# Raw first weights of the later pairs of feature tiles loaded behind the third chunk's attention output

## The chip, the cores and the metric

The kernel runs on one core of one Trainium2 chip. The metric is the device time of one execution in microseconds (us), and the median of several executions is compared. Five engines work side by side, each on its own list of instructions in a fixed order: PE (TensorE: matrix products, with PEld for its weight loads), DVE (VectorE), ACT (ScalarE), POOL (GpSimd) and SP (SyncE). POOL and SP mainly issue transfers (DMA) here, each on a queue of its own.

## What is computed

Two identical layers, one after the other, on a sequence of 2048 positions of width 576. Each layer is sliding dilated attention (32 heads of 18, 8 keys at distance 2) and a feed-forward part with SiLU over 4608 hidden features, each with a layer norm ahead and a residual around it. Both layers use the same weights.

```python
qkv = (x @ wqkv)                                   # 576 -> 3*576, 32 heads of 18
idx = pos[:, None] - arange(8)[None, :] * 2        # 8 keys, every second position back
logits = einsum("bhsd,bhswd->bhsw", q, k[idx]) * 18**-0.5   # masked where idx < 0
o = einsum("bhsw,bhswd->bhsd", softmax(logits), v[idx])
A(x) = o @ wo
B(x) = silu(x @ w1) @ w2                           # 576 -> 4608 -> 576
x = x + A(layernorm(x));  x = x + B(layernorm(x))  # layer 1
x = x + A(layernorm(x));  x = x + B(layernorm(x))  # layer 2
```

## The kernel before

**Chunks and stages.** The positions are cut into four chunks of 512, so that two layers make eight steps, `s` = 0 to 7 (`s` = 2 is the third chunk of the first layer). A step has an attention (four units of 8 heads, mostly DVE work: products L837 and L870, sums L841 and L877/L878, softmax L850 to L857), a projection with `wo`, and a feed-forward part.

**The projection** (`project`) takes the attention output `o` in four tiles of 128 positions. DVE writes each as two fp16 parts (L898 the high one, L492 the low one) into a buffer `yh`, of which there are two. From step 2 on SP then turns the tile with a transposing transfer (L509) into `oT`, shown as `yo`, of which there are two as well. The list `flipped` collects these turns. PE multiplies each turned tile with `wo` in two halves (L925), each into one of three PSUM banks (`z0`, `z1`, `misc0`), and DVE adds a half to the residual (L927), which frees the bank.

**The feed-forward part** of the first two chunks works on 36 single feature tiles: a product per tile (L1385, 14 matmuls into one of the same three banks), SiLU and split on ACT and DVE (L1387, L1389, L1392), and a second product per two tiles (L1345, four blocks of 12 weight steps). From the third chunk on the tiles are taken in 18 pairs with a fast form of the first product (`ffn_pairs`, L1232): seven products a pair instead of eight. For it the input is first made into seven forms (`forms`, L1179 to L1203), and the first weights of each pair into seven sums and differences in two fp16 parts.

**Making these weights** is `prepare(q)`, once for each of 18 pairs. POOL loads the raw weights of the pair with eight transfers (L1072, L1076; 768 KB) into one of two buffers `wr` (shown as `wq`). DVE forms four sums (L1083), ACT writes the high parts (L1091), DVE the low parts (L1098), and POOL stores both blocks of the pair into `wfs` in device memory (L1103). SP later reads `wfs` back, seven transfers per pair and chunk (L1108).

**What sets the order.** The program is first collected as operations, each with an engine, an estimated duration, what it reads and writes, a priority (lower goes first) and possibly operations that it must come after (`after=`). `Plan.order()` then plays this through with estimated durations and buffers and writes down one fixed order, which all engines follow. Priorities are mostly the step number: feed-forward work on DVE has `s - 0.5`, the attention `s - 1.0`, and `prepare` has `PREP = 0.9`, that is behind the second chunk's feed-forward work (0.5) and ahead of the third chunk's attention (1.0). Within the loop over steps, `front(s + 1)` records the attention, the projection and the forms of the next step.

Of the kernel before, what the change touches and what calls it, by code (L numbers as in the profile page):

```python
# [17 lines left out]
P = 128  # L18
# [23 lines left out]
NP = NFT // 2  # L42
# [4 lines left out]
W2N = 11  # L47
FAR = 6
PREP = 0.9
PS = 0.45  # L50
S2 = 2
TWICE = {6: 0, 7: 0}
# [22 lines left out]
class Plan:  # L75
# [18 lines left out]
    def op(self, eng, dur, fn, reads=(), writes=(), prio=0.0, nbytes=0, table=None, after=(), lanes=1, lag=0.0):  # L94
        o = Op()
        o.lag = lag
        o.eng, o.dur, o.fn, o.prio, o.seq, o.nbytes, o.table = eng, dur, fn, prio, len(self.ops), nbytes, table
        o.outs, o.end, o.lanes = [], None, lanes
        deps = set(after)
        for k in reads:  # L100
            if k in self.writer:
                deps.add(self.writer[k])
        for k in writes:
            if k in self.writer:
                deps.add(self.writer[k])
            deps.update(self.readers.get(k, ()))
        for k in reads:
            self.readers.setdefault(k, []).append(o)
        for k in writes:
            self.writer[k] = o  # L110
            self.readers[k] = []
        deps.discard(o)
        o.deps = deps
        o.n = len(deps)
        for d in deps:
            d.outs.append(o)
        o.bufs = []
        for k in (*reads, *writes):
            b = k[0] if isinstance(k, tuple) else k
            if isinstance(b, Buf) and b not in o.bufs:  # L120
                o.bufs.append(b)
                b.left += 1
                if b.turn is None:
                    b.turn = self.named[b.tag]
                    self.named[b.tag] += 1
        self.ops.append(o)
        return o
# [152 lines left out]
def sliding_attention_silu_ffn(ctx: ExitStack, tc: tile.TileContext, x, wqkv, wo, w1, w2, out):  # L280
# [6 lines left out]
    op = S.op  # L287

    def fl(t):
        return t.rearrange("p a b -> p (a b)")  # L290
# [8 lines left out]
    def T(b):  # L299
        if isinstance(b, tuple):  # L300
            return T(b[0])[:, b[1]]
        return S.tags[b.tag][b.slot]
# [152 lines left out]
    wsc = accw[:, 0:NP, :]  # L455
# [65 lines left out]
    turned, held, flipped = [], [], []  # L521
# [539 lines left out]
            nc.vector.tensor_scalar(dz, r12.rearrange("p (q f) i -> p q f i", f=2)[:, :, 0, 0], 2.0 / LNX, None, op0=ALU.mult)  # L1061
        op("DVE", 1.0, fn, [("s12", f) for f in range(NFT)] + [("sh", 2, g) for g in range(len(G2))], ["wsc"], -0.5)

    def prepare(q, prio):

        w, v = Buf("wr"), Buf("ws")

        def load():
            t = T(w)
            for h in range(2):  # L1070
                for k in range(2):
                    nc.gpsimd.dma_start(t[:, h:4:2, k, :], w1[h * KH + k * P:h * KH + (k + 1) * P, 2 * q * P:(2 * q + 2) * P].rearrange(  # L1072
                        "p (f c) -> p f c", f=2))
                for f in range(2):
                    v = w1[h * KH + 2 * P:(h + 1) * KH, (2 * q + f) * P:(2 * q + f + 1) * P]
                    nc.gpsimd.dma_start(t[:, h + 2 * f, 2, :], bass.AP(tensor=v.tensor, offset=v.offset, ap=[[0, 4], *v.ap]))  # L1076
        op("POOL", 4.8, load, ["wsc"], [w], prio, nbytes=P * 12 * P * 4, lanes=8)

        def sums():
            t, u = T(w), T(v)  # L1080
            for o, a, b, f in ((u[:, 0], t[:, 2], t[:, 3], ALU.add), (u[:, 1], u[:, 0], t[:, 0], ALU.subtract),
                               (t[:, 2], t[:, 0], t[:, 2], ALU.subtract), (u[:, 2], t[:, 1], u[:, 1], ALU.subtract)):
                nc.vector.tensor_tensor(o, a, b, op=f)  # L1083
        op("DVE", 2.0, sums, [w], [w, v], prio)
        for x, r0, r1, g in ((w, 0, 4, Buf("wg")), (v, 4, 7, Buf("wh"))):
            n = r1 - r0

            def hi(x=x, g=g):
                d, t = T(g), T(x)
                for k0, k1, c in ((0, 2, 0), (2, 3, 1)):  # L1090
                    nc.scalar.activation(d[:, :, k0:k1, :].rearrange("p a b c -> p a (b c)"),  # L1091
                                         t[:, :, k0:k1, :].rearrange("p a b c -> p a (b c)"), AF.Copy, scale=wsc[:, q, c:c + 1])
            op("ACT", 0.4 * n, hi, [x, "wsc"], [(g, 0)], prio)

            def lo(x=x, g=g):
                d, t = T(g), T(x)
                for o, k0, k1 in ((3, 0, 2), (2, 2, 3)):
                    nc.vector.scalar_tensor_tensor(  # L1098
                        d[:, :, o:o + k1 - k0, :].rearrange("p a b c -> p a (b c)"),
                        t[:, :, k0:k1, :].rearrange("p a b c -> p a (b c)"), wsc[:, q, 0:1],  # L1100
                        d[:, :, k0:k1, :].rearrange("p a b c -> p a (b c)"), op0=ALU.mult, op1=ALU.subtract)
            op("DVE", 0.43 * n, lo, [x, (g, 0)], [(g, 0)], prio)
            op("POOL", 0.57, lambda g=g, r0=r0, r1=r1: nc.gpsimd.dma_start(  # L1103
                wfs[q][:, r0 * KB:r1 * KB], T(g).rearrange("p i a b -> p (i a b)")), [(g, 0)], [("wfs", q, r0 // 4)], prio, nbytes=P * n * KB * 2)
# [347 lines left out]
    def load_x(s, prio, ahead=None, spilt=False, into=None):  # L1452

        lay, c = divmod(s, NC)
        halves = [Buf("x") for _ in range(2)] if into is None else [Buf(into)]
        xs = [(halves[j // 2], j % 2) if into is None else (halves[0], j) for j in range(NJ)]
        for j in range(NJ):
            src = (lambda j=j: x_rows(x, c, j)) if lay == 0 else (lambda j=j: (xe if spilt else xd)[c][j])
            if ahead and lay == 0:
                op("POOL", 0.54, lambda j=j, src=src: nc.gpsimd.dma_start(T(xs[j]), src()), [], [xs[j]], prio,  # L1460
                   nbytes=P * D * 4, after=ahead)
            else:
                op("SP", 0.41, lambda j=j, src=src: nc.sync.dma_start(T(xs[j]), src()), [("xe" if spilt else "xd", c, j)] if lay else [],
                   [xs[j]], prio, nbytes=P * D * (4 if s else 5), after=ahead or ())
        return xs
# [3 lines left out]
    def front(s):  # L1469
        X[s] = load_x(s, s - 1.0 if s else -20)  # L1470
        if s == 0:
            no_keys()
            xT = layer_norm(X[0], -20, "xa", 3, PE_LN[0])
            x1 = layer_norm(load_x(1, -8.5, gate[0:1]), -8.5, "xb", False, PE_LN[1])
            x2 = layer_norm(load_x(2, -2.0, gate[3:4]), -2.0, "xb", True, PE_LN[2])

            def more(u, w):
                qkv_ahead(1, u, x1, w)
                qkv_ahead(2, u, x2, w)
                ahead.append((u, w))  # L1480
            o = attention(0, xT, raw_wq, more)
            x3 = layer_norm(load_x(3, -1.2, gate[11:12]), -1.2, "xa", 2, PE_LN[3])
            for u in (2, 0, 1, 3):
                store_wq(u, ahead[u][1], PACE_WQ[u])
            for u in (0, 1, 3, 2):
                qkv_ahead(3, u, x3, ahead[u][1] if u != 2 else load_wq(2, -0.95))
            raw_wo()
        else:
            o = attention(s, None, None)
        project(s, o, X[s])  # L1490
        XT[s] = layer_norm(X[s], s - 1.0, "xb", s == 1, s == 0) if s < S2 else forms(X[s], s - 1.0, ("ya", "yc"))
# [25 lines left out]
    def turn(s):  # L1517
        XT[s] = forms(load_x(s, s - 1.0, spilt=True), s - 1.0, into="ye")
        X[s] = load_x(s, s - 1.0, spilt=True)
# [14 lines left out]
    for s in range(NL * NC):  # L1534

        if s < S2:
            ffn(s, XT[s], X[s])
        else:
            ffn_pairs(s, XT[s], X[s], TWICE.get(s, len(G2)))
        if s == 0:  # L1540
            for q in range(NP):
                prepare(q, PREP)
        if s == 2:
            op("POOL", 0.55, lambda: nc.gpsimd.dma_start(wos, fl(T(WO))), [(WO, k) for k in range(10)], ["wos"], 2.0, nbytes=P * 20 * D, after=flipped[-1:])
        if 2 <= s < NC:
            layer_norm(X[s], AN[s + NC] + 0.0, None, False, own=True, keep=xn[s - 2])
        if s < NC - 1:
            front(s + 1)
        if s == NC - 1:
            norm(NC)  # L1550
            attend(NC)
            norm(NC + 1)
            turn(NC)
            attend(NC + 1)
            norm(NC + 2)
            attend(NC + 2)
            norm(NC + 3)
        if NC <= s < NL * NC - 1:
            turn(s + 1)
        if s == NC:  # L1560
            attend(NC + 3)
            for q in range(NP):
                prepare_second(q, NC + 1 + PS, attended[-1:])
    for o in S.order():
# [28 lines left out]
```

## Time and profile before

| what | value |
|---|---|
| median of 3 runs | 2123.3 us (2121.58 to 2124.65) |
| profiled execution, own time | 2119.38 us |
| its span in the trace | 2117.6 us |
| PE busy | 2088.3 us, 99% of the span |
| DVE busy | 1754.9 us, 83% |
| ACT busy | 1025.8 us, 48% |
| POOL busy | 388.5 us, 18% |
| transfers | 489.07 MB, 231 GB/s |

The profiled execution's own time is 1.78 us above its span, and 3.9 us below the median of the timed runs. A row of a timeline gives the start, the duration, the engine, the line, the operation, what it writes `<-` what it reads, the count, and in brackets the idle time of the engine just before it and what ended it. SPq, DVEq and the like are the queues that issue an engine's instructions.

### The profile page before, as it was taken

To read this page: it belongs to the slowest core of one execution; us is meant where nothing else is said; L and a number is where in the kernel's file an instruction comes from. 1 tells how busy PE (TensorE), PEld (TensorE's weight loads), DVE (VectorE), ACT (ScalarE), POOL (GpSimd) and SP (SyncE) were. 2 spreads that over 40 slices of the span, in tenths; PEclk is the share of its full clock that TensorE was granted. 3 is DMA by queue.
4 is the path that set the end of the run, shared out by engine and by line. 5 is a ranking of instruction groups with operands and counts; after the bars stand their busy time and mean duration, and the time that the engine had idled before them with its cause. 6 is when DMAs were issued, how large, how long until landed. Compare 5 with 4: busy or idle time off the path is not lost.

```text
span 2117.6 us, 41751 instructions
## 1 busy us (share of the span) xinstructions
PE 2088.3 (99%) x16017; PEld 1539.5 (73%) x16017; DVE 1754.9 (83%) x2861; ACT 1025.8 (48%) x1857; POOL 388.5 (18%) x628
## 2 busy tenths in 40 slices
PE   8999999999999999999999999999999999999999
PEld 4556556665566888877786777777788888888887
DVE  8899999999876998679997978986996748766665
ACT  7555787644345454434434433434444545444442
POOL 2133566343322232011111001001000000000000
PEclk9999999999999999999999999999999999999999
DMA  6477777687989889886677896786989999779772
GB/s 188 146 212 256 236 258 248 214 243 221 250 206 297 264 275 252 210 261 189 177 220 208 218 273 195 217 225 185 247 256 302 330 258 290 218 213 272 221 210 76
DMA packets 377632, 489.07 MB, mean 231 GB/s; under 512 B 150600, under 2 KB 300724, under 8 KB 373080
## 3 DMA queue, kind: packets, MB, share of 16 engines
q1 hardware_dynamic: 332456, 336.85, 56.9%
q0 software_dynamic: 42960, 148.45, 21.8%
q8 instruction: 125, 2.05, 0.4%
q10 hardware_dynamic: 2016, 1.11, 0.2%
q14 instruction: 75, 0.61, 0.1%
HBM read 350.96 MB, written 86.85 MB: 207 GB/s over the span
## 4 chain that ended last, share of the span: by engine, by line
PE 87%; DVE 6%; DMA 4%; ACT 1%; issue 1%; SPq 0%; POOL 0%; ACTq 0%; DVEq 0%
PE acc L1345 19%; PE z L1232 16%; PE misc L1232 10%; PE z L735 9%; PE acc L1322 9%; PE z L1385 7%; PE acc L1409 4%; PE misc L1345 4%; PE misc L735 3%; PE z L925 3%; PE misc L1385 2%; PE misc L925 1%; DMA kvs<-kvs 1%; DMA yo<-yh 1%; DVE prs L837 1%
## 5 line engine op out<-in xcount | busy, mean ns | idle before, releaser
L1232 PEld LDWEIGHTS <-w 128*128 128x128 f16 x5292 | 516.5, 98 | 74.5 <-issue 2.5
L1345 PE MATMUL acc<-w,h 128*128 128x320 f16 (+2 forms) x3780 | 548.2, 280 | 2.3 <-DVE x L1353 2.3
L1345 PEld LDWEIGHTS <-h 128*128 128x128 f16 x4320 | 407.6, 98 | 122.3 <-issue 3.3
L1232 PE MATMUL z<-xb,w 128*128 128x256 f16 x3213 | 405.0, 273 | 0.5 <-DVE wq L1239 0.5
L1232 PE MATMUL misc<-xb,w 128*128 128x256 f16 x2079 | 272.2, 273 | 1.1 <-DVE wq L1239 0.8
L735 PEld LDWEIGHTS <-xa 128*128 128x128 f16 x1344 | 130.8, 98 | 115.5 <-issue 6.7
L837 DVE TENSOR_TENSOR prs<-qts,kvs 128x2304 f32<-128x2304 f32 x64 | 163.4, 2554 | 18.8 <-DMA kvs<-kvs 17.0
L870 DVE TENSOR_TENSOR prs<-kvs,pe 128x1152 f32<-128x1152 f32 x128 | 170.3, 1352 | 1.0
L841 DVE TENSOR_REDUCE lg<-prs 128x128 f32<-128x2304 f32 x64 | 163.1, 2548 | 0.9
L735 PE MATMUL z<-wq,xa 128*128 128x432 f16 x840 | 160.2, 346 | 2.1 <-ACT h L748 2.1
L1345 PE MATMUL misc<-w,h 128*128 128x384 f16 x540 | 139.7, 326 | 0.0
L877 DVE TENSOR_TENSOR prs<-prs 128x1152 f32<-128x1152 f32 (+1 forms) x128 | 135.1, 1056 | 3.2
L1331 DVE SCALAR_TENSOR_TENSOR x<-acc,d2x,x 128x576 f32<-128x576 f32 (+1 forms) x85 | 68.7, 810 | 57.2 <-PE acc L1322 56.6
L1385 PEld LDWEIGHTS <-w 128*128 128x128 f16 x588 | 57.9, 99 | 74.2 <-issue 7.6
L1409 PE MATMUL acc<-w,h 128*128 128x288 f16 x864 | 108.4, 286 | 1.9 <-DVE h L1392 1.1
L1409 PEld LDWEIGHTS <-h 128*128 128x128 f16 x864 | 83.7, 98 | 25.2 <-DVE h L1392 1.4
L1385 PE MATMUL z<-xb,w 128*128 128x512 f16 x420 | 93.9, 379 | 0.7 <-DVE w L1011 0.6
L1385 PE MATMUL z<-xb,wq 128*128 128x512 f16 x420 | 92.8, 379 | 1.7 <-ACT h L1387 1.7
L1236 ACT ACTIVATE wq<-z 128x256 f32<-128x256 f32 x107 | 40.8, 382 | 103.8 <-PE z L1232 103.7
L1387 ACT ACTIVATE h<-z,d 128x512 f32<-128x512 f32 x60 | 40.9, 682 | 94.9 <-PE z L1385 86.4
L1322 PEld LDWEIGHTS <-h 128*128 128x128 f16 x756 | 74.0, 98 | 17.6
L925 PEld LDWEIGHTS <-yo 128*128 128x128 f16 x672 | 65.7, 98 | 18.6 <-issue 1.9
(322 smaller groups left out, 3369.0 us busy)
## 6 DMA issues: line engine op xcount, KB each, us to landing
w<-wfs SPq DMA_DIRECT2D x756, 160.0 KB, 3.9
w<-w2s SPq DMA_DIRECT2D x180, 288.0 KB, 4.9
wq<-wqs SPq DMA_DIRECT2D x17, 1080.0 KB, 6.6
kvs<-kd POOLq DMA_DIRECT2D x8, 1584.0 KB, 8.4
w<-w1s SPq DMA_DIRECT2D x36, 320.0 KB, 5.9
wfs<-xa POOLq DMA_DIRECT2D x18, 640.0 KB, 4.6
kvs<-wts SPq DMA_DIRECT2D x80, 144.0 KB, 3.1
w2s<-w POOLq DMA_DIRECT2D x36, 288.0 KB, 4.7
```

Of the source, the lines that this page charges most:

```text
L735: nc.tensor.matmul(T(m)[:, :3 * UC], a, b, start=n == 0, stop=n == len(pl) - 1)
L837: nc.vector.tensor_tensor(T(pr), T(qt)[:, j:j + 2, None, :].to_broadcast([P, 2, W, UC]), win(T(kv), j, 2), op=ALU.mult)
L841: nc.vector.tensor_reduce(T(lg)[:, j:j + 2].rearrange("p a w h -> p (a w h)"), T(pr).rearrange("p a w (h d) -> p (a w h) d", d=DH), axis=A ...
L870: nc.vector.tensor_tensor(T(pr)[:, a].rearrange("p w (h d) -> p w h d", d=DH), v, T(pe)[:, j + a, :, :, None].to_broadcast([P, W, UH, DH]) ...
L877: nc.vector.tensor_tensor(t[:, :, 0:h, :], t[:, :, 0:h, :], t[:, :, h:2 * h, :], op=ALU.add)
L925: nc.tensor.matmul(T(m)[:, 0:288], a, b, start=n == 0, stop=n == len(pl) - 1)
L1232: nc.tensor.matmul(t, w[:, u, :], v[:, r, :], start=first and m == 0, stop=m == 6, skip_group_check=True)
L1322: nc.tensor.matmul(T(acc)[:, j, 0:KH], T(hb[t])[:, a, row[k], j * P:(j + 1) * P], T(wb[k, t])[:, w, :], start=k in (5, 1, 2) and t == 0 an ...
L1331: nc.vector.scalar_tensor_tensor(v, T(acc)[:, a:b, 0:KH], d2x[:, g:g + 1], v, op0=ALU.mult, op1=ALU.add)
L1345: nc.tensor.matmul(T(fa[b])[:, o:o + 2 * n].rearrange("p (a b) -> p a b", a=2), h(f, a, j), w(f)[:, :, v, c:c + n], start=q == f == m == 0 ...
L1385: nc.tensor.matmul(T(z), v, u, start=m == 0, stop=m == len(pl) - 1)
L1409: nc.tensor.matmul(T(acc)[:, h, 0:288], T(hb[q])[:, a, j * P:(j + 1) * P], T(wbs[q][0])[:, h, w, :], start=q == 0 and m == 0, stop=q == n ...
```

## The change

A constant `HELD = 5` is new. `prepare` gets a parameter `after` that is handed to its loading operation. Pairs 0 to 4 are recorded where all 18 were. Pairs 5 to 17 are recorded one step later, behind the third chunk's `front(2)`, and their load on POOL must come after `flipped[-1]`, which is then the turn of the fourth tile of the third chunk's attention output. Priority and all else of `prepare` stay.

```diff
+HELD = 5
...
-    def prepare(q, prio):
+    def prepare(q, prio, after=()):
...
-        op("POOL", 4.8, load, ["wsc"], [w], prio, nbytes=P * 12 * P * 4, lanes=8)
+        op("POOL", 4.8, load, ["wsc"], [w], prio, nbytes=P * 12 * P * 4, lanes=8, after=after)
...
         if s == 0:
-            for q in range(NP):
+            for q in range(HELD):
                 prepare(q, PREP)
...
         if s < NC - 1:
             front(s + 1)
+        if s == 1:
+            for q in range(HELD, NP):
+                prepare(q, PREP, flipped[-1:])
```

Lines of the changed kernel stand one higher than before from the constant on. Since the order is planned, one new dependence moves instructions on every engine. Three places show it.

DVE, at the end of the third chunk's attention (`prs` holds the weighted values, `xa` the prepared weights, `yh` the first tile for the projection). Before:

```order
L870 TENSOR_TENSOR prs<-kvs,pe_82 128x1152 x2
L1098 SCALAR_TENSOR_TENSOR xa<-wq,accw,xa 128x4x256
L1098 SCALAR_TENSOR_TENSOR xa<-wq,accw,xa 128x4x128
L1098 SCALAR_TENSOR_TENSOR xa<-wq,accw,xa 128x3x256
L1098 SCALAR_TENSOR_TENSOR xa<-wq,accw,xa 128x3x128
L877 TENSOR_TENSOR prs<-prs 128x2x576
L877 TENSOR_TENSOR prs<-prs 128x2x288
L878 TENSOR_TENSOR o<-prs 128x2x144
L898 TENSOR_SCALAR yh<-o,so 128x576
```

Now, at the same place:

```order
L871 TENSOR_TENSOR prs<-kvs,pe_82 128x1152 x2
L878 TENSOR_TENSOR prs<-prs 128x2x576
L878 TENSOR_TENSOR prs<-prs 128x2x288
L879 TENSOR_TENSOR o<-prs 128x2x144
L899 TENSOR_SCALAR yh<-o,so 128x576
L871 TENSOR_TENSOR prs<-kvs,pe_82 128x1152 x2
L878 TENSOR_TENSOR prs<-prs 128x2x576
L878 TENSOR_TENSOR prs<-prs 128x2x288
L879 TENSOR_TENSOR o<-prs 128x2x144
L493 SCALAR_TENSOR_TENSOR yh<-o,so,yh 128x512
L493 SCALAR_TENSOR_TENSOR yh<-o,so,yh 128x64
L899 TENSOR_SCALAR yh<-o,so 128x576
```

The four low parts of pair 5 are gone from here, and so are its four sums a little earlier; both now stand behind the projection.

POOL, in the same stretch (`wfs_218` and `wfs_219` are the prepared weights of pairs 4 and 5, `kd_275` and `kd_276` the keys and values of the fourth chunk's first two units, `qd` their queries). Before, with the raw loads of pairs 4 and 5 ahead of it and those of pairs 6 and 7 behind it:

```order
L1103 DMA wfs_218<-xa 128x2560
L1103 DMA wfs_218<-xa 128x1920
L779 DMA kvs<-kd_275 128x3168
L781 DMA qts<-qd_267 128x576
L1103 DMA wfs_219<-xa 128x2560
L1103 DMA wfs_219<-xa 128x1920
L779 DMA kvs<-kd_276 128x3168
L781 DMA qts<-qd_268 128x576
L1072 DMA wq<-in_B_w_dram 128x2x128 x2
L1076 DMA wq<-in_B_w_dram 128x1x128 x2
```

Now, with the raw load of pair 4 alone ahead of it and those of pairs 5 and 6 behind it:

```order
L780 DMA kvs<-kd_275 128x3168
L782 DMA qts<-qd_267 128x576
L1104 DMA wfs_218<-xa 128x2560
L1104 DMA wfs_218<-xa 128x1920
L780 DMA kvs<-kd_276 128x3168
L782 DMA qts<-qd_268 128x576
L1073 DMA wq<-in_B_w_dram 128x2x128 x2
L1077 DMA wq<-in_B_w_dram 128x1x128 x2
```

The last two rows are the first that wait for the fourth turn. From here on the stores lag by one pair: the store of `wo`'s fp16 parts, which follows that of pair 6 before, now follows that of pair 5.

DVE, at the projection of the fourth chunk (L1239 and L1270 are the feed-forward part's sums and splits). Before, the low parts of pair 15 come ahead of the last weighted values:

```order
L1098 SCALAR_TENSOR_TENSOR xa<-wq,accw,xa 128x3x128
L1239 TENSOR_TENSOR yo<-z_95,yo 128x256
L1270 SCALAR_TENSOR_TENSOR h<-h,sh_303 128x1024
L870 TENSOR_TENSOR prs<-kvs,pe_82 128x1152
L1239 TENSOR_TENSOR yo<-z_94,yo 128x256
L870 TENSOR_TENSOR prs<-kvs,pe_82 128x1152
L1239 TENSOR_TENSOR yo<-misc_96,yo 128x256
L877 TENSOR_TENSOR prs<-prs 128x2x576
L877 TENSOR_TENSOR prs<-prs 128x2x288
L878 TENSOR_TENSOR o<-prs 128x2x144
L898 TENSOR_SCALAR yh<-o,so 128x576
```

Now they come behind the first two tiles for the projection:

```order
L899 TENSOR_SCALAR yh<-o,so 128x576
L493 SCALAR_TENSOR_TENSOR yh<-o,so,yh 128x512
L493 SCALAR_TENSOR_TENSOR yh<-o,so,yh 128x64
L899 TENSOR_SCALAR yh<-o,so 128x576
L493 SCALAR_TENSOR_TENSOR yh<-o,so,yh 128x512
L493 SCALAR_TENSOR_TENSOR yh<-o,so,yh 128x64
L1099 SCALAR_TENSOR_TENSOR xa<-wq,accw,xa 128x4x256
L1099 SCALAR_TENSOR_TENSOR xa<-wq,accw,xa 128x4x128
L1271 SCALAR_TENSOR_TENSOR h<-h,sh_303 128x1024
L1099 SCALAR_TENSOR_TENSOR xa<-wq,accw,xa 128x3x256
```

The raw load of pair 17 uses the buffer that pair 15 frees here, so it too moves, from ahead of the fourth chunk's turns to the time of its third and fourth turn. On PE the projection of the third chunk stood one tile at a time between products of single feature tiles; now its first two tiles stand together ahead of a second product (L1345), and the last two stand behind this and one first product (L1385). Every engine has as many instructions as before.

## The prediction, made before the changed kernel was run

> **What bounds the kernel now.** I read the page first: the busy shares and the chain of work that ended last.
>
> ```profile
> PE 2088.3 (99%) x16017; PEld 1539.5 (73%) x16017; DVE 1754.9 (83%) x2861; ACT 1025.8 (48%) x1857; POOL 388.5 (18%) x628
> PE 87%; DVE 6%; DMA 4%; ACT 1%; issue 1%; SPq 0%; POOL 0%; ACTq 0%; DVEq 0%
> ```
>
> TensorE is the bound, 99% of the span. The change leaves its instructions as they are, so it can only win idle time of PE or a lowered clock, and only lose by new idle time. The busy time by stretches shows where there is any to win:
>
> ```profile
> core 0: us, PE busy (x) PEld busy (x) DVE busy (x) ACT busy (x) POOL busy (x), PEclk, DMA share, GB/s
> 320.00:570.00 250.00, 250.00 (x1680) 159.70 (x1678) 241.29 (x344) 138.61 (x211) 101.88 (x164) 1.00 0.78 240
> 570.00:603.00 33.00, 28.61 (x185) 18.25 (x183) 22.53 (x43) 12.00 (x16) 3.11 (x5) 0.90 0.77 189
> 603.00:2080.00 1477.00, 1471.35 (x11989) 1158.02 (x11987) 1173.99 (x1919) 653.13 (x1217) 161.02 (x260) 1.00 0.84 238
> ```
>
> Of the 33 us around the third chunk's projection PE idles 4.39, and its granted clock is 0.90; in the 1477 us after it all other waits together are 5.65 us. The timeline of PE has the place, and the chain of waits what led to it:
>
> ```profile
> 573.18 1.88 PE L925 MATMUL z<-wos,yo 128*128 128x288 f16 x14
> 579.44 5.36 PE L1385 MATMUL misc<-xb,w 128*128 128x512 f16 x14 [4.39 <-DVE x L927]
> 588.07 3.19 PE L1385 MATMUL misc<-xb,w 128*128 128x512 f16 x14
> 562.23 16.19 DMA yo<-yh
> 578.44 0.52 DVE yh L898
> 578.96 0.44 DVE x L927
> 588.24 3.02 PE misc L1385 x14
> ```
>
> After the first tile's two halves PE wants bank `misc` back. The addition L927 that frees it stands on DVE behind L898, the fourth tile's copy, and that copy needs the `yh` buffer from which the second tile is still being turned: 16.19 us from issue to landing. After the gap the same 14 matmuls take 5.36 us instead of 3.02. So the wait costs 4.39 + (5.36 - 3.02) = 6.73 us.
>
> Why the turn is late, from the timelines of SP and POOL and the queues' shares in 570 to 579:
>
> ```profile
> 558.68 2.19 SPq L509 DMA_TRANSPOSE yo<-yh  x1
> 562.23 14.15 SPq L509 DMA_TRANSPOSE yo<-yh  x2
> 554.21 0.54 POOL L779 DMA_DIRECT2D kvs<-kd  x1 [5.10 <-DVE prs L870]
> 562.71 0.72 POOL L1076 DMA_DIRECT2D wq<-in_B_w_dram  x1 [3.11 <-DMA kvs<-kd]
> 573.80 0.70 POOL L1076 DMA_DIRECT2D wq<-in_B_w_dram  x1 [1.03 <-DMA wq<-in_B_w_dram]
> q0 software_dynamic: 499, 0.74, 68.4%
> q1 hardware_dynamic: 1241, 0.31, 30.4%
> DMA to landing us min/median/max: 3.3/3.3/3.3
> ```
>
> From 555 to 574.5 POOL issues the raw loads of pairs 6 and 7. Its queue (q0) holds 68.4% of the engines' time while the turn is under way; the last row is the turn of the last tile, issued at 588.27 with that queue quiet: 3.3 us.
>
> **The change, part by part.**
>
> *The wait at the third chunk's projection.* Pairs 6 and 7 are no longer loaded before the fourth turn, and pair 5's DVE work leaves the end of the attention:
>
> ```profile
> 536.60 2.08 DVE L1083 TENSOR_TENSOR wq<-wq 128x384 f32<-128x384 f32 x4
> 544.87 3.40 DVE L1098 SCALAR_TENSOR_TENSOR xa<-wq,accw,xa 128x1024 f16<-128x1024 f32 x4
> 550.86 0.52 DVE L898 TENSOR_SCALAR yh<-o,so 128x576 f16<-128x576 f32 x1
> 559.91 0.95 DVE L492 SCALAR_TENSOR_TENSOR yh<-o,so,yh 128x512 f16<-128x512 f32 x2
> ```
>
> That is 2.08 + 3.40 = 5.48 us of DVE. The second tile's parts, done at 560.86, should be done some 6 us sooner, near 555. In the new order PE takes four projection halves from about 565.6 on (one second product, 5.88 us, earlier than the 571.46 of before). The second turn has 10 us until then, and the fourth bank use, three halves later, 15 us; 3.3 us are needed in quiet, and even with the fourth chunk's key load (`kd_276`, from 549 at the earliest; before, POOL waited 8.5 us for it, 554.21 to 562.71) it lands near 562. The wait should go whole. Bounds: 0 gained if it comes back at its old length, and 6.73 + 5.65 = 12.4 if all later waits went too. I take 6.73, as the rows price it.
>
> The Trainium skill, page "DMA: Bandwidth & Descriptors", section "Queues, rings and completion order", speaks against so large a share for the raw loads: a transfer engine takes turns between the queues that have work, packet by packet. By that a neighbour queue about doubles the 3.3 us of a turn, and the other 9.6 of 16.19 would belong to the turn's own queue and remain. The second turn would then land 12.9 us after 555, at 568, the addition would follow near 571, and the fourth half, due at 570.7, would lose about 0.6: a sum of 6.1 instead of 6.7. The trace cannot decide it, since no turn of this stage runs beside one queue alone.
>
> *The moved work on DVE, ACT and POOL.* Per pair 5.48 us on DVE; by the order DVE is one pair behind from here to the fourth chunk's projection. What hides it is DVE's idle time:
>
> ```profile
> 600.00:640.00 40.00, 40.00 (x254) 24.13 (x252) 27.94 (x70) 19.31 (x43) 15.11 (x22) 1.00 0.92 225
> 640.00:680.00 40.00, 40.00 (x273) 25.94 (x272) 23.05 (x37) 20.45 (x36) 12.45 (x19) 1.00 1.03 286
> 840.00:880.00 40.00, 40.00 (x345) 32.88 (x343) 31.09 (x96) 16.95 (x39) 2.87 (x4) 1.00 0.84 242
> 880.00:920.00 40.00, 38.89 (x320) 30.56 (x318) 23.26 (x67) 13.03 (x32) 2.97 (x5) 1.00 0.88 212
> ```
>
> 12.06 + 16.95 = 29.0 us are free before 680 and 25.7 between 840 and 920; ACT and POOL have half or more. Cost 0. If DVE had none, 5.48 would come back.
>
> *The deadline of `wfs`.* The last pair's store and its use:
>
> ```profile
> 845.94 0.54 POOL L1103 DMA_DIRECT2D wfs<-xa  x1 [4.25 <-DVE xa L1098]
> 663.78 0.93 PE L1232 MATMUL misc<-xb,w 128*128 128x256 f16 x7
> 880.84 0.93 PE L1232 MATMUL z<-xb,w 128*128 128x256 f16 x7
> 897.94 2.24 PE L1232 MATMUL z<-xb,w 128*128 128x256 f16 x19
> ```
>
> The stretch from the first of these products to the next chunk's, 663.78 to 897.94, gives 13.0 us a pair; the last pair's products start at 880.84, 34.9 us after the store is issued. A lag of one pair leaves 22. Cost 0; its bound is 0 as long as the lag stays below 34.9.
>
> *The new wait on POOL.* Behind the held load stand only the store of pair 5 and what follows from it; the key loads now stand ahead of it. SP and PE do not wait for POOL there. Cost 0.
>
> *The fourth chunk's projection.* Before, its turns ran in quiet:
>
> ```profile
> 810.76 0.70 POOL L1076 DMA_DIRECT2D wq<-in_B_w_dram  x1 [0.79 <-DMA wfs<-xa]
> 828.19 1.88 PE L925 MATMUL misc<-wos,yo 128*128 128x288 f16 x14
> 831.81 4.73 SPq L509 DMA_TRANSPOSE yo<-yh  x2
> 841.75 1.88 PE L925 MATMUL z<-wos,yo 128*128 128x288 f16 x14
> ```
>
> The last raw load (pair 17) is issued by 811.5. In the new order it follows pair 15's low parts, which stand behind the second tile's copy: about 827 to 833 on the scale of before, right across the third turn. That turn cannot be issued before the first tile is multiplied (831.8 of before, 3.6 us after the first half). In the new order the third tile is due 6.9 + 9.0 us after the first half (four halves of 1.715; five products L1232 and three quarters of a second product between), so the turn has 12.3 us. With one pair's load beside it instead of two and a key load I expect 3.3 to 12 us. Cost 0 as likeliest, 4 us if it takes 16.2 again, 6.2 with the clock.
>
> *All other waits* are dealt anew, since the order changes to the end. The longest kinds before, with their total, count and longest:
>
> ```profile
> PE acc L1345 <- DVE x L1353: 2.3, 5, 0.7
> PE misc L925 <- DVE wq L1239: 1.8, 1, 1.8
> ```
>
> They were 5.65 us in 1477; I take the same again, with an error of about its own size to either side.
>
> **Sum.** 2119.38 - 6.73 = 2112.65 for the profiled execution. The median of the runs lies 3.92 above it: 2123.3 - 6.7 = 2116.6.
>
> **The rivals.**
>
> *The wait moves to the fourth chunk's projection.* For it: the raw load of pair 17 now falls on the third turn. Against: it is one pair's load, not two. Price 4 to 6.2, net gain 0.5 to 2.7: about 2121.5, within 0.2%. It decides once that turn takes over 12.3 us.
>
> *The change does not do what it says: the turn is late for another reason.* For it: two weight loads of SP's own queue stand between the first two turns, and `kd_276` is issued ahead of them in both orders. Against: the last turn, with w2 and w1 loads around it too, took 3.3. Price 6.73, so 2123.3, no change. It needs a second turn that lands after 571.
>
> *Slower: the lag of one pair reaches the second layer.* The norm of the first chunk's second layer waits for the last `wfs` store, and in the new order its loads stand about three pairs further down SP's list. If DVE's 25.7 us free between 840 and 920 do not take up the lag, the second layer's attention comes up to one pair, 13.0 us, late for the fifth step's input. Against: its first projection stands only one pair later on PE, and the fifth step about two and a half pairs behind that. Price up to 13.0: 2116.6 + 13.0 = 2129.6. It decides for slower from 11 us on.
>
> **How the numbers follow.** About 0.2%, 4.2 us, is what a measurement of this kernel tells from no change. Chances: the forecast 0.69 (its own range 2112 to 2119.5, with 0.04 of it above the line of 2119.1), the wait at the fourth chunk's projection 0.15, no effect 0.08, slower 0.08. So faster 0.65, same 0.04 + 0.15 + 0.08 = 0.27, slower 0.08. The range of 8 in 10 takes in the forecast with most of its good side (2112, from the bound of 12.4 rounded inward), the second case and the no-change case to 2123.5.
>
> **What would show it.** Right: in the profile after, PE has no wait of over 1 us between the first L925 of the third chunk and the second L1385 behind it, the granted clock there is 1.00, the turns L509 of that chunk take under 8 us, and L898 waits for no DMA. The last `wfs` store comes 0 to 10 us later relative to the first L1232. Wrong: a wait of several us at L925 or L1385 near the fourth chunk's projection behind `yo<-yh`; or PE waiting for DVE forms (`xb`) at the start of a feed-forward part; or new waits behind L1239 and L1353 that sum to more than 5 us above the 5.65 of before.

## The result: slower by 0.8%, and the profile after

Over five runs each, the changed kernel takes 2137.77 us (2134.26 to 2139.51) and the kernel before 2121.58 us (2116.62 to 2124.65). The ratio is 1.008, with a 95% interval of 1.0059 to 1.0100. The profiled execution took 2139.51 us, its span is 2137.7 us, 20.1 more than that of before. Ratios further down are to the kernel before as timed beside each run (medians of 2119.9 to 2120.8 us). One execution of `real6`, 2413.69 us at a granted clock of 0.851, is slow for a cause that is not known and is left out of the medians and ratios.

The page, busy time of PE and the chain that ended last:

```profile
PE 2095.3 (98%) x16017; PEld 1542.6 (72%) x16017; DVE 1754.5 (82%) x2861; ACT 1025.8 (48%) x1857; POOL 389.0 (18%) x628
PE 84%; DMA 6%; DVE 6%; issue 1%; ACT 1%; SPq 1%; POOL 0%; DVEq 0%; ACTq 0%; POOLq 0%
```

PE has the same 16017 matmuls and is busy 7.0 us longer. The rest of the 20.1, 13.1 us, is idle time, and the chain has more DMA in it, 6% instead of 4%. The busy time by stretches shows where:

```profile
core 0: us, PE busy (x) PEld busy (x) DVE busy (x) ACT busy (x) POOL busy (x), PEclk, DMA share, GB/s
320.00:564.00 244.00, 244.00 (x1631) 155.12 (x1629) 234.85 (x335) 134.52 (x204) 94.34 (x152) 1.00 0.74 230
564.00:590.00 26.00, 21.75 (x154) 15.22 (x152) 11.57 (x23) 3.11 (x4) 1.42 (x2) 0.93 0.80 157
590.00:635.00 45.00, 45.00 (x285) 27.22 (x284) 29.01 (x70) 17.81 (x34) 14.32 (x21) 1.00 0.74 192
635.00:660.00 25.00, 17.75 (x91) 9.88 (x89) 12.78 (x26) 10.99 (x22) 6.90 (x10) 0.80 0.97 229
660.00:700.00 40.00, 37.02 (x255) 25.08 (x254) 24.46 (x35) 19.98 (x35) 9.12 (x14) 0.96 1.03 261
```

The idle time at the third chunk's projection is still there (4.25 us, clock 0.93). Two new places stand behind it: 635 to 660 (7.25 us idle, clock 0.80) and 660 to 700 (2.98 us, clock 0.96). Before, PE was busy in the whole of 603 to 680. What PE waited for from 540 to 720:

```profile
PE misc L1346 <- ACT h L1390: 7.2, 1, 7.2
PE misc L1233 <- DMA xb<-yh: 3.0, 1, 3.0
PE misc L926 <- DVE x L928: 2.5, 1, 2.5
PE z L926 <- DMA yo<-yh: 1.7, 1, 1.7
```

I laid each trace beside that of before by the number of matmuls done, at points where the same ones had run on both. Each column of the table below says how much a kernel lost against the kernel before in one stretch (minus: gained). The kernels are explained under the experiments; each row is one profiled execution. The last column is by how much the first raw load beside the turns of the third chunk's forms was issued ahead of the first of these turns (minus: behind it). It is the load of pair 8 in the order of before and in that of `HELD = 6`, and of pair 7 in that of `HELD = 5`; the rows for it are shown further down for six kernels. "Cut" means that this load was among those cut down. Times are on the scale of before.

| kernel | to 540 | 540 to 588, projection | 588 to 673, forms | 673 to 965 | 965 to 1243 | 1243 to 1780 | to the end | load ahead of turn |
|---|---|---|---|---|---|---|---|---|
| changed | -0.9 | -0.55 | +15.12 | +1.0 | +3.7 | -2.8 | +4.5 | -4.1 |
| real5 | +3.3 | -6.73 | +17.56 | +2.4 | +1.1 | -2.4 | +4.3 | -4.1 |
| thin56_after | +3.0 | -6.72 | +14.51 | +5.3 | +1.9 | -3.3 | +4.3 | -4.1 |
| thin78_after | -0.7 | -2.12 | +7.53 | +1.8 | +1.1 | -3.3 | +4.6 | cut |
| thin_after | +1.1 | -6.73 | +0.01 | +1.5 | -0.7 | -3.3 | +2.1 | cut |
| held6 | 0.0 | +3.20 | +11.10 | +7.9 | +0.8 | -2.5 | +0.9 | -5.5 |
| real6 | -0.1 | -6.73 | +11.16 | -0.9 | +0.3 | -3.3 | +4.5 | -5.5 |
| thin_before | +2.1 | -6.73 | 0.00 | -0.1 | +0.2 | -0.9 | +0.2 | cut |
| thin67_before | -0.8 | -6.73 | 0.00 | +0.1 | -0.5 | -1.8 | -0.2 | +5.9 |
| wait2_before | -1.4 | -6.73 | 0.00 | 0.0 | +0.1 | 0.0 | +1.2 | +5.9 |
| wait1_before | +2.3 | -6.73 | 0.00 | +0.2 | +0.3 | -2.3 | -0.3 | +5.9 |

So 15.1 of the 20.1 us lie in one stretch of 85 us right behind the projection. From 673 to 965, PE also waits for a load of `wqs`, 2.9 us in `thin56_after` and 3.4 in `held6` against 0.7 in the changed kernel; no experiment aimed at this wait.

**Why the projection's wait stayed.** POOL's timeline, SP's turns and DVE's fourth copy in the changed kernel:

```profile
548.57 0.55 POOL L780 DMA_DIRECT2D kvs<-kd  x1 [12.59 <-DVE prs L871]
549.65 1.43 POOL L1073 DMA_DIRECT2D wq<-in_B_w_dram  x2
559.25 1.56 POOL L1073 DMA_DIRECT2D wq<-in_B_w_dram  x2 [0.56 <-DMA wq<-in_B_w_dram]
568.39 1.42 POOL L1077 DMA_DIRECT2D wq<-in_B_w_dram  x2 [4.54 <-DMA wq<-in_B_w_dram]
568.34 10.89 SPq L510 DMA_TRANSPOSE yo<-yh  x2
570.00 0.52 DVE L899 TENSOR_SCALAR yh<-o,so 128x576 f16<-128x576 f32 x1 [5.32 <-DMA yo<-yh]
```

and the second turn in the chain of waits:

```profile
556.06 13.92 DMA yo<-yh
```

The raw loads of pairs 5 and 6 are issued from 549.65 to 569.8, right behind the key load, while the third and fourth turns are issued from 568.34 on. The "held" loads did not wait for the fourth turn at all. They run beside the second turn, just as those of pairs 6 and 7 did before, and it takes 13.92 us, from 556.06 to 570.00. The list of what each POOL instruction waits for says why (DMASW are semaphores that count landed transfers of POOL, DMAHW those of SP's transfers):

```
338 L780 DMA kvs<-kd_276 128x3168 [waits DMAHW5_49,DMASW2_49,DVE_49]
339 L782 DMA qts<-qd_268 128x576 [waits DMAHW6_49,DMASW3_49]
340 L1073 DMA wq<-in_B_w_dram 128x2x128 [waits DMASW4_49]
341 L1073 DMA wq<-in_B_w_dram 128x2x128 [waits DMASW5_49]
```

`after=` is only a constraint of the plan. It decides where an instruction stands in its engine's list. On the chip an instruction waits for what it reads and overwrites, and the raw load reads nothing of the turn. The sentence above that the last two of POOL's rows "wait for the fourth turn" is wrong: the plan waited, the chip did not.

**Where the new 15 us come from.** The chain of waits in the forms' stage:

```profile
616.87 3.35 PE z L1386 x16
620.22 4.55 DMA xb<-yo
624.77 16.67 DMA xb<-yh
641.52 0.44 ACT yh L1194
641.97 0.12 ACT yh L1195
642.09 0.58 ACT h L1388
642.69 0.73 ACT h L1390
```

and three rows of ACT's timeline from within it:

```profile
629.89 0.44 ACT L1194 ACTIVATE yo<-o 128x288 f16<-128x288 f32 x1 [4.85 <-DMA xb<-yo]
639.10 0.44 ACT L1194 ACTIVATE yo<-prs 128x288 f16<-128x288 f32 x1 [8.65 <-DMA xb<-yo]
641.52 0.44 ACT L1194 ACTIVATE yh<-o 128x288 f16<-128x288 f32 x1 [1.86 <-DMA xb<-yh]
```

The turns of the forms take long, one of them 16.67 us, so the buffers they read come free late. ACT stands in line on them three times with the next form's high part (L1194), and behind that in ACT's list stands the SiLU of a single feature tile (L1388, L1390), which PE's second product needs. It is the same pattern as at the projection, with ACT in DVE's place. Beside it POOL loads pairs 7 and 8. Their first load and the first turn, in the changed kernel and then in the kernel before:

```profile
617.02 1.44 POOL L1073 DMA_DIRECT2D wq<-in_B_w_dram  x2
612.93 5.02 SPq L1204 DMA_TRANSPOSE xb<-yh  x2
```

```profile
611.50 1.44 POOL L1072 DMA_DIRECT2D wq<-in_B_w_dram  x2
617.42 2.54 SPq L1203 DMA_TRANSPOSE xb<-yh  x2
```

Before, the loads start 5.9 us ahead of the first turn and all are issued by 623.9; the last four of the eight turns are issued after that. Now they start 4.1 us behind it and go on to 633.0, and only the last two turns are issued later.

### The profile page after: what moved, and what is told of

It reads as the page before. It is cut to its first block, busy times and chain, and to the rows that moved or that the text cites. A ratio compares the mean times of both kernels' runs of the same rounds, so it can differ in the third digit from the quotient of the medians.

```text
span 2137.7 us, 41726 instructions
## 1 busy us (share of the span) xinstructions
PE 2095.3 (98%) x16017; PEld 1542.6 (72%) x16017; DVE 1754.5 (82%) x2861; ACT 1025.8 (48%) x1857; POOL 389.0 (18%) x628
## 4 chain that ended last, share of the span: by engine, by line
PE 84%; DMA 6%; DVE 6%; issue 1%; ACT 1%; SPq 1%; POOL 0%; DVEq 0%; ACTq 0%; POOLq 0%
PE acc L1346 19%; PE z L1233 15%; PE misc L1233 10%; PE acc L1323 8%; PE z L736 8%; PE z L1386 6%; PE misc L1346 4%; PE acc L1410 4%; PE misc L736 4%; PE z L926 3%; PE misc L1386 2%; DMA xb<-yh 1%; PE misc L926 1%; DMA w<-wfs 1%; DMA qts<-qd 1%
## 5 line engine op out<-in xcount | busy, mean ns | idle before, releaser
L736 PE MATMUL z<-wq,xa 128*128 128x432 f16 x770 | 146.3, 346 | 1.8 <-ACT h L749 1.7
L1388 ACT ACTIVATE h<-z,d 128x512 f32<-128x512 f32 x60 | 40.8, 681 | 96.1 <-PE z L1386 89.7
L1323 PEld LDWEIGHTS <-h 128*128 128x128 f16 x756 | 74.0, 98 | 17.6
L736 PE MATMUL misc<-wq,xa 128*128 128x432 f16 x406 | 80.4, 351 | 5.6 <-ACT qts L806 4.0
```

The costliest lines, as they stand in the source:

```text
L736: nc.tensor.matmul(T(m)[:, :3 * UC], a, b, start=n == 0, stop=n == len(pl) - 1)
L1323: nc.tensor.matmul(T(acc)[:, j, 0:KH], T(hb[t])[:, a, row[k], j * P:(j + 1) * P], T(wb[k, t])[:, w, :], start=k in (5, 1, 2) and t == 0 an ...
```

## The experiments

Cutting a load keeps every instruction in its place and takes away only most of what its transfers move, so these kernels leave out most of the weights concerned. The edit, with the pairs concerned in place of `q >= 5`:

```diff
+            n = 2 if q >= 5 else 32
...
-                    nc.gpsimd.dma_start(t[:, h:4:2, k, :], w1[h * KH + k * P:h * KH + (k + 1) * P, ...
+                    nc.gpsimd.dma_start(t[0:4 * n, h:4:2, k, :], w1[h * KH + k * P:h * KH + k * P + 4 * n, ...
```

**All raw loads from pair 5 on cut, in both orders.**

> The changed kernel, the raw loads of pairs 5 to 17 cut to 8 of 128 partitions (most of their weights are left out), order unchanged. Theory A (the raw loads hold up the turns): the losses of PE at 570 (6.0), 636 (10.3) and 680 (4.8 us) go, those near 1220 (+4.3) and 1813 (+4.5) stay, since they stand after the last raw load: about 2117. Rival B (the new order itself, ACT and DVE waiting in line, makes the waits): within 5 us of 2138.

> The kernel before, the raw loads of pairs 5 to 17 cut to 8 of 128 partitions (most of their weights are left out), order unchanged. Theory A: the wait of 6.7 us at the third chunk's projection goes, about 2115. Rival B: 2122.

Measured: 2117.1 us (11 runs, ratio to before 0.9988, 0.9976 to 1.0001) and 2111.86 us (0.9958, 0.9944 to 0.9972; 3 us less than expected). All that is left of PE's waits from 540 to 720 in the changed order with cut loads:

```profile
PE acc L1347 <- DVE x L1355: 0.6, 1, 0.6
```

Theory A holds. Without the raw loads the stretch of the forms costs +0.01 in the changed order and the projection gains its 6.73 in both. The new order is harmless there by itself; the transfers that it moves do the damage. In the profiled executions the two orders end within 0.8 us of each other. The medians are 5.2 us apart; the runs of the changed order scatter from 2113.09 to 2124.44 and the profiled one, 2113.43, is near their low end, so what the changed order still costs in other runs stays open.

**Single loads cut.**

> The changed kernel, only the raw loads of pairs 7 and 8 cut to 8 of 128 partitions (most of their weights are left out). Theory A: they are what stretches the turns of the forms between 613 and 641; PE's wait of 7.2 us there and the slow matmuls behind it go, 10.3 us, the rest stays: 2127 to 2129. Rival B (ACT's order, or the weight loads of the turns' own queue): 2135 to 2139.

> The changed kernel, only the raw loads of pairs 5 and 6 cut to 8 of 128 partitions (most of their weights are left out). Theory A: they are what holds up the second turn in the changed kernel; its 6.0 us go, the losses at the forms (10.3 and 4.8 us) stay: 2130 to 2133. Rival: with them out of the way the pairs behind run ahead and miss the turns of the forms too: 2118 to 2124.

> The kernel before, only the raw loads of pairs 6 and 7 cut to 8 of 128 partitions (most of their weights are left out). Theory A: these two loads are the whole cause of the wait of 6.7 us: 2113 to 2116. Rival B (the key load and the weight loads hold the turn up as well): 2118 to 2121.

Measured: 2129.25 us (1.0039, 1.0026 to 1.0052), 2134.16 us (1.0070, 1.0057 to 1.0083) and 2111.73 us (0.9956, 0.9944 to 0.9968). Pairs 7 and 8 cut: ACT's wait of 7.2 us is gone, and the next one grew, from 3.0 to 5.3:

```profile
PE misc L1234 <- DMA xb<-yh: 5.3, 1, 5.3
PE misc L926 <- DVE x L928: 2.5, 1, 2.5
```

Against the changed kernel the median is 8.5 us lower and the span 11.1 us shorter. Pairs 5 and 6 cut: the projection gains 6.72, the forms keep their wait of 7.0, and the sum is 3.6 us less than that of the changed kernel, 1 us above what was expected. Pairs 6 and 7 cut in the order of before: 6.73, all of the wait, and 1.3 us less in all than expected. So the projection's wait goes with the two raw loads beside it, in either order, and the 7.2 us at the forms with those of pairs 7 and 8. The later wait at the forms (3.0, then 5.3) goes when all later raw loads are cut too, as in `thin_after`; which of them it belongs to was not tried. The waits also differ from one execution to the next: in `thin78_after` the projection cost 1.6 us less than in the changed kernel, though its own two loads were whole.

**The hold made real.** POOL copies one element of the turned tile ahead of the load, so it does wait:

```diff
+        last = turnedT[-1][0] if q == HELD else None
...
         def load():
+            if last:
+                nc.gpsimd.tensor_copy(pace, T(last)[0:1, 0, 0:1])
```

> The changed kernel with the hold made a wait: POOL copies one element of the fourth turned tile ahead of the raw load of pair 5; order otherwise that of the changed kernel. Theory A (in the changed kernel the hold is only a place in the order; the raw loads of pairs 5 and 6 still run beside the second turn): the second turn lands in under 8 us, PE's waits of 1.7 + 2.5 us and the slow matmuls at the third chunk's projection go, 6.0 us; the loads of pairs 5 and 6 start near 577 and later ones keep colliding with the turns of the forms, where the 10.3 us stay or grow: 2128 to 2138. Rival B (the turn is late by its own queue): the turn still takes 13 us, 2138 or more.

Measured: 2134.82 us (1.0066, 1.0051 to 1.0081). The timelines of POOL and SP, and then PE's waits to 720:

```profile
579.26 0.17 POOL L1073 CAST pace<-yo 1x1 f32<-1x1 f16 x1 [25.46 <-DMA yo<-yh]
579.75 1.43 POOL L1077 DMA_DIRECT2D wq<-in_B_w_dram  x2 [0.32 <-issue]
615.00 1.44 POOL L1077 DMA_DIRECT2D wq<-in_B_w_dram  x2
610.92 5.02 SPq L1208 DMA_TRANSPOSE xb<-yh  x2
```

```profile
PE misc L1350 <- ACT h L1394: 8.1, 1, 8.1
PE misc L1237 <- DMA xb<-yh: 4.4, 1, 4.4
```

POOL waits 25.46 us, the projection gains 6.73, and the forms take 17.6 back. So even the change as its words describe it is slower: it clears one set of turns and lays the next loads across the following one.

**One pair later.**

> The changed kernel with HELD = 6, the hold again only a place in the order. POOL's list is that of the kernel before up to the last third of the loads, so by theory A the loads of pairs 6 and 7 still run beside the second turn, PE waits 4 to 5 us for the addition there as in the kernel before, and no 7 us wait appears at the forms if the loads of pairs 8 and 9 are still issued ahead of them (before 613): 2119 to 2125. If they slip behind the forms' first turn by 4 us or more, as in the changed kernel: 2130 to 2138.

> HELD = 6, and POOL really waits for the fourth turn ahead of the raw load of pair 6. Theory A: no wait at the third chunk's projection (6.7 us gone), but the loads of pairs 6 and 7 start near 580 instead of 555, those of pairs 8 and 9 later by some 10 to 15 us and so beside the turns of the forms: PE loses about 10 us there, 2122 to 2130. Rival (a real hold gives what the change is said to do): 2115.

Measured: 2140.92 us (4 runs; 1.0092, 1.0079 to 1.0105) and 2133.93 us (5 runs, 2124.38 to 2138.22; 1.0059, 1.0041 to 1.0076). Both are above what was expected. The trace of `real6` is of its fastest run; what the others lose besides is open. The first loads and turns, of `held6` and then of `real6`:

```profile
629.71 1.44 POOL L1073 DMA_DIRECT2D wq<-in_B_w_dram  x2
624.22 2.74 SPq L1204 DMA_TRANSPOSE xb<-yh  x2
```

```profile
619.79 1.44 POOL L1077 DMA_DIRECT2D wq<-in_B_w_dram  x2
614.30 2.71 SPq L1208 DMA_TRANSPOSE xb<-yh  x2
```

In `held6` the loads of pairs 6 and 7 still meet the second turn (PE waits 7.3 us, more than before), and in both kernels the later loads slip 5.5 us behind the forms' first turn, and 11 us are lost there. The order of POOL's list was no guide to this: it is that of before for these pairs. What moved is DVE's work for them, and with it the stores that stand ahead of the next loads.

**A shorter real wait in the order of before.** It keeps every instruction of before and adds one copy:

```diff
+            if q == 6:
+                nc.gpsimd.tensor_copy(pace, T(turnedT[1])[0:1, 0, 0:1])
```

> The kernel before with one real wait: POOL copies one element of the second turned tile of the third chunk ahead of the raw load of pair 6; order otherwise that of the kernel before. Theory A: the second turn lands by 568, the addition behind the fourth copy is no longer late, and the 6.7 us of PE go; the raw loads start near 567 instead of 555 and should land near 580, when DVE's sums of pair 6 want them (583.9 of before, some 5 us sooner without the wait), so up to 3 us can come back there: 2114 to 2118 beside 2121. Rival C (the loads only move the collision: the sums of pair 6 hold up DVE's additions, or the turns of the forms are met again as in the changed kernel): 2121 or more.

> As wait2_before, but POOL waits for the first turned tile of the third chunk instead of the second, so that the raw loads of pairs 6 and 7 are issued from about 561 to 575, again beside the second turn. Theory A (what counts is that no raw load runs beside the second turn): the second turn is late again, by less than before since the loads start some 6 us later; PE loses 2 to 7 us there: 2115 to 2120. Rival D (any pause of the loads does, since the key load is then out of the way): 2112, as with the wait for the second turn.

Measured: 2112.47 us (0.9961, 0.9949 to 0.9973) and 2112.88 us (0.9965, 0.9953 to 0.9978). Both beat the kernel before and the changed one by more than was expected of theory A, and `wait2_before` lies within 0.8 us of the kernel without the loads of pairs 6 and 7. POOL in `wait2_before`, with its store of pair 6, and the first turn of the forms:

```profile
567.67 0.29 POOL L1073 CAST pace<-yo 1x1 f32<-1x1 f16 x1 [13.80 <-DMA yo<-yh]
568.16 1.43 POOL L1076 DMA_DIRECT2D wq<-in_B_w_dram  x2 [0.20 <-issue]
583.99 0.58 POOL L1107 DMA_DIRECT2D wfs<-xa  x1 [4.37 <-DVE xa L1102]
603.36 1.44 POOL L1076 DMA_DIRECT2D wq<-in_B_w_dram  x2
609.28 2.54 SPq L1207 DMA_TRANSPOSE xb<-yh  x2
```

The loads start 12.9 us later than before (568.16 against 555.27) and the store of pair 6 is issued 7.9 us earlier (583.99 against 591.87), because DVE is no longer stuck. The later loads keep their lead over the forms' turns, and nothing comes back. `wait1_before` has the time that rival D gives, but it does not separate the theories. Its copy stood from 568.65 to 571.2, so the raw loads began only at 571.17, and by the semaphore events of its trace the second turn landed at 572.46: they met no more than its last 1.3 us. So it stays open whether the raw loads would hold up that turn without the key load ahead of them. At the forms, from 602 to 645, POOL of the changed kernel loads no keys, and the turns there are late all the same.

## Why the prediction was wrong, point by point

- *What bounds the kernel, and the price of the wait* were right. The prediction took 4.39 + 2.34 = 6.73 us; seven kernels gain 6.73 and one 6.72 at this place.
- *The cause of the late turn* was right: cutting two raw loads gives back all of PE's wait. By the Trainium skill, page "DMA: Bandwidth & Descriptors", section "Queues, rings and completion order", engines alternate packet by packet between queues. The prediction read this as a doubling of the turn, which gave 6.1 and left 9.6 us of the turn to its own queue, 12.9 in all. The trace does not agree with the doubling: nothing of the wait was left, and in `wait2_before`, with no raw load beside it, the second turn took at most 7.6 us (560.05 to POOL's copy at 567.67). In the row of 570 to 579 above, a packet of q0 holds an engine 5.6 times as long as one of q1 (68.4 / 499 against 30.4 / 1241), so alternation by packets need not mean equal time.
- *The step that failed: "pairs 6 and 7 are no longer loaded before the fourth turn", and "the new wait on POOL".* There is no new wait. POOL loaded pairs 5 and 6 in the same place. The DVE part of the step was right: the second tile's parts were done by 553.2 (forecast 555), PE reached the first half at 564.71 (565.6). But the turn took 13.92 us, and the gain was 0.55 instead of 6.73. A small misreading stands beside it: the 8.5 us from 554.21 to 562.71 are not a wait of POOL, which issued other transfers meanwhile and then waited 3.11. The rival that the change does not do what it says had the right outcome at this place, but for another reason (the turn's own queue, the key load); `thin56_after` and `thin67_before` rule these out as causes by themselves.
- *The second step that failed: the moved work "cost 0", since DVE has room.* DVE does have room. But a pair's work on DVE ends in stores, and the next raw loads stand behind these. Which turns they meet is what the move changed, and the forms' turns, some 45 us further on, had no term of their own and no rival. They lay in the stretch whose waits all together were given 5.65 us, and only the list of signs names them (PE waiting for `xb`). They cost 15.1 us.
- *Right at cost 0:* the fourth chunk's projection and the deadline of `wfs`. The turns there, the last store and the products that stand where those at 880.84 stood before:

```profile
833.97 2.77 SPq L510 DMA_TRANSPOSE yo<-yh  x2
847.35 4.71 SPq L510 DMA_TRANSPOSE yo<-yh  x2
879.87 0.54 POOL L1104 DMA_DIRECT2D wfs<-xa  x1 [0.92 <-DVE xa L1099]
894.84 1.69 PE L1233 MATMUL z<-xb,w 128*128 128x256 f16 x14
```

  The store keeps 15.0 us, where 22 were forecast.
- *All other waits* were given 5.65 us to either side. From 673 to the end they add 6.4. The 4.5 us near the end come back in four further kernels of these orders (+4.3 to +4.6; `thin_after` has 2.1, `held6` 0.9); DVE waits there for a load of the residual. Which moved row causes it was not tried. The 3.7 us before 1243 do not come back (1.1, 1.9, 1.1) and are that one execution's.

## What to carry to other kernels

A dependence that only a planner knows moves instructions in a list; it holds nothing on the chip. Before pricing a hold, look at what the instruction itself waits for, and if a transfer must wait for another engine, give its issuer an operation that reads the result. And when work is shifted, follow its transfers to the next stage: a large load beside small turning transfers costs whoever stands in line behind the turn, so a hold should be as short as the turn it protects. (Here the hold that paid was short and also kept the order of before; the two were not tried apart.)

## What was not expected of the hardware

A turn at the projection that takes 3.3 us in quiet took 13.92 and 16.19 us beside the key load and raw loads. At the forms one took 16.67 us, and at most 7.2 with the raw loads of pairs 7 and 8 cut (`thin78_after`, 622.42 to ACT's next use of its buffer at 629.65). Waits of PE cost about one and a half times their length: 4.39 us idle cost 6.73, 7.25 cost 10.3 in all (the 37 matmuls behind took 6.95 us instead of 4.66), 2.98 cost 4.8, each with a lowered granted clock around it (0.90, 0.80 and 0.96 in the stretches shown). Kernels with the order of before, whose lists are equal that far, stood -1.4 to +2.3 us from it already at 540 us.
